# Attention feeding a SwiGLU block: four half steps of the third tile ahead of the first tile's outputs, activations in five half buffers, one v scale behind the weight casts

## The chip, the cores and the metric

One Trainium2 chip, one of its cores. The metric is the device time of one execution of the whole kernel, in microseconds (us). Every program is run several times; a profiled execution is one more run whose instructions were recorded.

## The reference

Two parts follow each other. First, a decaying linear attention over 4 sequences of 768 positions with 8 heads of width 64. It goes block by block; every block of a sequence needs the state that the block before it has left. Second, a gated feed-forward block over the 3072 x 512 result.

```python
for b in range(nb):                                   # blocks of one sequence, in order
    intra = einsum('bhic,bhjc->bhij', qb, kb) * Dmask  # decay lam ** (i - j), causal
    intra = einsum('bhij,bhjd->bhid', intra, vb)
    inter = einsum('bhid,bhde->bhie', qb * lam_pow, kv_state)
    out[:, :, sl] = intra + inter
    kv_state = lam_block * kv_state + einsum('bhsd,bhse->bhde', kb * rev_pow, vb)
x = out.transpose(0, 2, 1, 3).reshape(3072, 512)
g = x @ w_gate                                        # 512 -> 1536
result = (g * sigmoid(g) * (x @ w_val)) @ w_out       # 1536 -> 512
```

Inputs and output are float32; inside, the kernel works in bfloat16 with float32 accumulation.

## The kernel before

**Tiles and groups.** The 3072 rows are six *tiles* of 512 rows. A tile has two *groups* of 256 rows, so there are twelve groups, g0 to g11; group g belongs to tile g // 2. Attention works by group, the feed-forward block by tile.

**What a group needs.** k, q and v are loaded as float32 (`load_group`, on SyncE's queue SP). `cast_scaled` makes bfloat16 of k on ScalarE (L258) and of q, with its decay, on VectorE (L260), and then issues a transposing DMA on SP (L251). `v_scale` writes v with its decay on GpSimd (L238). `upd_mm` (L382) multiplies scaled v with k on TensorE, `upd_copy` copies the result out of PSUM on ScalarE (tile `ups`, L404), and `state` runs a chain of small additions and copies on GpSimd (L421 to L432) that gives the group its incoming states `kvn` and leaves `kvs` for the next block. `scores` (L326, or L352 from group 6 on) and its masks on VectorE (`ssb`) give the causal part. `core_a` (L461) and `core_b` (L474) accumulate the group's result, and `evac` copies it into the tile's input `xt` (L486), two copies, either one each on VectorE and ScalarE (`SPLIT`) or both on ScalarE, as for groups 4 and 5.

**The feed-forward block.** A *step* (t, fc) takes 128 of the 1536 inner columns of tile t: four matmuls by `w_gate` (L514), a Silu on ScalarE (`sil`, L518), four matmuls by `w_val` (L528) and the product on VectorE (`h`, L531). A step can be a half step: group columns 0:2 or 2:4 alone, matmuls of 256 columns in place of 512. Tile 1 runs as half steps throughout (`s1a`, then `s1b`). `ffn_out(t, b)` makes 128 output rows: twelve matmuls of `h` by `w_out` (L547), a copy to `osb` (L549) and a DMA (L550). The very last one is done in two column slices, so that its copies and DMAs overlap. PSUM is eight banks taken in a ring.

**What sets the order.** It is written out by hand. `steps` lists the steps; `at(n, fn, ...)` hangs work behind step n; the loop at the end emits step after step and what hangs on it. Each engine runs its instructions in that order, and waits at the first whose inputs are not ready. DMAs wait on SP's queue in the same way. `ahead(g)` is `upd` (update matmul, copies, state chain) and `scores` of group g; `attend(g)` is `core_a(g)`, then `upd_mm`, `upd_copy` and `scores` of g + 1, then `core_b(g)`, then the state chain of g + 1.

**Around the change.** `w_out` comes as six pieces; `wo_cast` makes bfloat16 of them (L232), five on GpSimd and the last on ScalarE behind step (1, 10) of `s1b`. On GpSimd the scale of v of group 5 stands ahead of the last of its five casts. After the last step of tile 1 come the four outputs of tile 0 with the attention of group 5 between them; then the steps of tile 2, with `ahead(6)` behind step 2, the cast of group 7 behind step 3, its v scale behind step 4, `attend(6)` behind step 6, the cast of group 8 behind step 7, `attend(7)` behind step 10, and the outputs of tile 1 behind steps 0, 3, 7 and 9.

Of the kernel before, what the change touches and what calls it, by code (L numbers as in the profile page):

```python
# [9 lines left out]
BF16 = mybir.dt.bfloat16  # L10
# [9 lines left out]
@with_exitstack  # L20
def kernel(
    ctx: ExitStack,
    tc: tile.TileContext,
    q: bass.AP,
    k: bass.AP,
    v: bass.AP,
    lam: bass.AP,
    moe_w_gate: bass.AP,
    moe_w_val: bass.AP,
    moe_w_out: bass.AP,  # L30
    out: bass.AP,
):
    nc = tc.nc
    with tc.manual_schedule():
        _body(ctx, tc, nc, q, k, v, lam, moe_w_gate, moe_w_val, moe_w_out, out)


def _body(ctx, tc, nc, q, k, v, lam, moe_w_gate, moe_w_val, moe_w_out, out):
    B, H, S, D = q.shape
    HP = H // 2  # L40
    BLK = 128
    NBLK = S // BLK
    DM = H * D
    DFF = moe_w_gate.shape[1]
    MC = DM // 128
    FC = DFF // 128
    NG = NBLK * B // 2
    M = BLK // 2

# [8 lines left out]
    PB = B // 2  # L58
    groups = [(t % PB * 2 + j, t // PB) for t in range(NG // 2) for j in range(2)]

# [6 lines left out]
    vs_pool = ctx.enter_context(tc.tile_pool(name="vs", bufs=4))  # L67
    ssb_pool = ctx.enter_context(tc.tile_pool(name="ssb", bufs=2))
    xt_pool = ctx.enter_context(tc.tile_pool(name="xt", bufs=2))
    h_pool = ctx.enter_context(tc.tile_pool(name="h", bufs=2))  # L70
    sil_pool = ctx.enter_context(tc.tile_pool(name="sil", bufs=3))
    osb_pool = ctx.enter_context(tc.tile_pool(name="osb", bufs=3))
    kv_pool = ctx.enter_context(tc.tile_pool(name="kv", bufs=1))
# [5 lines left out]
    def bank():  # L79
        b = banks[ring[0] % 8]  # L80
        ring[0] += 1
        return b
# [8 lines left out]
    st = {}  # L91
# [54 lines left out]
    for b2 in range(2):  # L146
        ps = slice(b2 * M, b2 * M + M)
# [4 lines left out]
    for b2 in range(2):  # L152
        ps = slice(b2 * M, b2 * M + M)
# [46 lines left out]
    wv_sb = wpool.tile([128, MC, DFF], BF16, name="wv_sb")  # L200
    wo_sb = wpool.tile([128, FC, DM], BF16, name="wo_sb")
    wg_d = moe_w_gate.rearrange("(c p) f -> p c f", p=128)
# [163 lines left out]
    def upd_mm(g, up=None):  # L366
        b, i = groups[g]
        v_s = st[("vs", g)]
        up = up or [bank() for _ in range(2)]
        started = set()  # L370
        for s in range(2):
            for hp in range(HP):
                for r in range(2):
                    if g >= NAT0 and i == NG // B - 1 and 2 * s + r == 3:
                        continue
                    for h2 in range(2):
                        ps = slice(r * M, r * M + M)
                        h = 2 * hp + h2
                        if g >= NAT0 and r:
                            h = H - 1 - h  # L380
                        n = hp + (HP * s if g >= NAT0 else 0)
                        nc.tensor.matmul(up[r][h2 * 64:h2 * 64 + 64, n * D:n * D + D],  # L382
                                         st[("qk", g)][ps, 0, s, h * D:h * D + D],
                                         v_s[ps, 2 * hp + h2, s],
                                         start=(r, h2) not in started, stop=(s == 1 or g >= NAT0),
                                         skip_group_check=True)
                        started.add((r, h2))
        st[("up", g)] = up

    def upd_copy(g, parts=(0, 1)):  # L390
# [10 lines left out]
        for r in range(2):  # L401
            n = HP * D if g < NAT0 or (r == 1 and i == NG // B - 1) else 2 * HP * D
            u = kv_pool.tile([128, 2 * HP * D], FP32, name="ups", tag="ups", bufs=4)
# [6 lines left out]
    def state(g):  # L410
        b, i = groups[g]
        last = i == NG // B - 1
        us = st[("ups", g)]
# [76 lines left out]
    def core_a(g):  # L490
        st[("op", g)] = [bank() for _ in range(2)]
        inter(g, True)
        guard(g)

    def core_b(g, fns=(nc.scalar.copy, nc.scalar.copy)):
        run_later(len(later))
        intra(g, False)
        evac(g, fns)
# [19 lines left out]
        nc.scalar.activation(sil[:, 0:N], gp[:, 0:N], AF.Silu)  # L518

    def ffn_val(t, fc, b0=0, b1=B):  # L520
        if ("h", t) not in st:
            st[("h", t)] = h_pool.tile([128, FC, B, BLK], BF16, name="h", tag="h")
        h_sb, xt, sil = st[("h", t)], st[("xt", t)], st[("sil", t, fc, b0)]
        N = (b1 - b0) * BLK
        fs = slice(fc * 128, fc * 128 + 128)
        vp = bank()
        for mc in range(MC):
            nc.tensor.matmul(vp[:, 0:N], wv_sb[:, mc, fs],  # L528
                             xt[:, b0 // 2:b1 // 2, mc].rearrange("p g b n -> p g (b n)"),
                             start=(mc == 0), stop=(mc == MC - 1))  # L530
        nc.vector.tensor_tensor(out=h_sb[:, fc, b0:b1].rearrange("p b n -> p (b n)"),  # L531
                                in0=sil[:, 0:N], in1=vp[:, 0:N], op=ALU.mult)

    def ffn_fc(t, fc, b0=0, b1=B):
        ffn_gate(t, fc, b0, b1)
        ffn_val(t, fc, b0, b1)

    def ffn_out(t, b, last=False):
        h_sb = st[("h", t)]
        osb = osb_pool.tile([128, DM], FP32, name="osb", tag="osb")  # L540
        row = groups[2 * t + b // 2][0] * S + (groups[2 * t + b // 2][1] * 2 + b % 2) * BLK
        halves = ((0, DM // 2, nc.scalar.copy, nc.scalar), (DM // 2, DM, nc.vector.tensor_copy, nc.sync)) \
            if last else ((0, DM, nc.scalar.copy, nc.scalar),)
        for c0, c1, fn, eng in halves:
            ps = bank()[:, 0:c1 - c0]
            for fc in range(FC):
                nc.tensor.matmul(ps, h_sb[:, fc, b], wo_sb[:, fc, c0:c1],  # L547
                                 start=(fc == 0), stop=(fc == FC - 1))
            fn(out=osb[:, c0:c1], in_=ps)  # L549
            eng.dma_start(out=bass.AP(tensor=out.tensor, offset=out.offset + row * DM + c0,  # L550
                                      ap=[[DM, 128], [1, c1 - c0]]),
                          in_=osb[:, c0:c1])
# [6 lines left out]
    def attend(g):  # L559
        run_later(len(later))  # L560
        core_a(g)
        if g + 1 < NG:
            upd_mm(g + 1)
# [3 lines left out]
        core_b(g)  # L567
        if g + 1 < NG:
            later[:] = late
# [80 lines left out]
    inter(1, False)  # L650
    evac(1, SPLIT)
    ffn_val(0, 0, 0, 2)
    ring[0] = 6
    ffn_gate(0, 1, 0, 2)
    ffn_gate(0, 0, 2, 4)
    w_piece(6, 8)
    w_cast()
    ring[0] = 4
    ffn_val(0, 0, 2, 4)
    ffn_val(0, 1, 0, 2)  # L660
    ring[0] = 2
# [9 lines left out]
    def step(t, fc, b0=0, b1=B):  # L671
        steps.append((t, fc, b0, b1))
        return len(steps) - 1

    def at(n, fn, *a):
        plan.setdefault(n, []).append((fn, a))

    s0 = {fc: step(0, fc) for fc in range(2, FC - 1)}
    s0["11a"], s0["11b"] = step(0, FC - 1, 0, 2), step(0, FC - 1, 2, 4)
    at(s0[2], w_cast)  # L680
# [3 lines left out]
    at(s0[3], swapped_q_table)  # L684
    at(s0[4], w_cast)
    at(s0[4], state, 1)
    at(s0[4], load_group, 2, "v")
    at(s0[5], load_group, 3)
    at(s0[6], w_cast)
    at(s0[7], load_group, 4, "kq")  # L690
# [2 lines left out]
    at(s0[8], pe_transpose, 2, 0)  # L693
    at(s0[8], pe_transpose, 2, 1)
    at(s0[8], w_cast)
    at(s0[8], v_scale, 2, nc.gpsimd)
    at(s0[9], scores, 2)
    at(s0[9], run_later, 4)
    at(s0[10], upd_mm, 2)
# [8 lines left out]
    s1b = [step(1, fc, 2, 4) for fc in range(FC)]  # L708
# [19 lines left out]
    at(s1b[6], run_later, 2)  # L728
    at(s1b[6], wo_cast)
    at(s1b[6], wo_cast)  # L730
    at(s1b[6], v_scale, 5, nc.gpsimd)
    at(s1b[8], wo_cast)
    at(s1b[9], core_a, 4)
    at(s1b[10], core_b, 4)
    at(s1b[10], wo_cast, ACTC)
    at(s1b[11], ffn_out, 0, 0)
    at(s1b[11], ahead, 5)
    at(s1b[11], run_later, 3)
    at(s1b[11], ffn_out, 0, 1)
    at(s1b[11], core_a, 5)  # L740
    at(s1b[11], ffn_out, 0, 2)
    at(s1b[11], core_b, 5)
    at(s1b[11], cast_scaled, 6)
    at(s1b[11], load_group, 7)
    at(s1b[11], v_scale, 6, nc.gpsimd)
    at(s1b[11], ffn_out, 0, 3)

    outs = [(1, b) for b in range(4)]
    for t in range(2, NG // 2):
        sn = [step(t, fc) for fc in range(FC)]  # L750
        if t == 2:
            at(sn[2], ahead, 6)
        for j, g in ((3 if t == 2 else 0, 2 * t + 3), (7 if t == 2 else 6, 2 * t + 4)):
            if g < NG:
                at(sn[j], cast_scaled, g)
                if g + 1 < NG:
                    at(sn[j], load_group, g + 1)
                at(sn[1 + j], v_scale, g, nc.gpsimd)
        if t + 1 < NG // 2:
            at(sn[6 if t == 2 else 4], attend, 2 * t + 2)  # L760
            at(sn[10], attend, 2 * t + 3)
        for n, o in zip((0, 3, 7, 9), outs):
            at(sn[n], ffn_out, *o)
        outs = [(t, b) for b in range(4)]

# [40 lines left out]
```

## Time and profile before

| | us |
|---|---|
| median of 5 runs | 228.33 |
| lowest and highest of them | 227.96 and 229.51 |
| the profiled execution's own time | 228.64 |
| its span, from the first to the last instruction | 226.9 |
| busy in that span: TensorE | 219.3 |
| ScalarE | 107.2 |
| GpSimd | 89.9 |
| VectorE | 89.2 |

A profile line names the engine (PE is TensorE, PEld its weight loads, ACT ScalarE, DVE VectorE, POOL GpSimd, SP SyncE, with a q for the queue that issues DMAs), the source line, and the tiles it writes and reads. A timeline line has the start and the length in us first, then how many instructions it merges (x4), and in brackets the idle time of the engine before it and what ended that. The lengths of matmuls overlap, since they are pipelined: the distance from one start to the next is the better measure. The profiled execution lies 0.31 us above the median, and 1.74 us of its time lie outside the span.

### The profile page before, as it was taken

To read this page: it belongs to the slowest core of one execution; us is meant where nothing else is said; L and a number is where in the kernel's file an instruction comes from. 1 tells how busy PE (TensorE), PEld (TensorE's weight loads), DVE (VectorE), ACT (ScalarE), POOL (GpSimd) and SP (SyncE) were. 2 spreads that over 40 slices of the span, in tenths; PEclk is the share of its full clock that TensorE was granted. 3 is DMA by queue.
4 is the path that set the end of the run, shared out by engine and by line. 5 is a ranking of instruction groups with operands and counts; after the bars stand their busy time and mean duration, and the time that the engine had idled before them with its cause. 6 is when DMAs were issued, how large, how long until landed. Compare 5 with 4: busy or idle time off the path is not lost.

```text
span 226.9 us, 5902 instructions
## 1 busy us (share of the span) xinstructions
PE 219.3 (97%) x2443; PEld 118.4 (52%) x2443; DVE 89.2 (39%) x151; ACT 107.2 (47%) x209; POOL 89.9 (40%) x131
## 2 busy tenths in 40 slices
PE   8889999999998999999999999999999999999994
PEld 3556455878864444454544544544544444444443
DVE  2664357685834214444253262253242123222200
ACT  6868585754662446364454453453533423322221
POOL 6676747642795303977463092192150000000000
PEclk9999999999999999999999999999999999999999
DMA  6999999899997678878988749915101101101122
GB/s 195 344 360 376 367 336 326 218 248 301 342 259 187 190 173 211 192 178 203 216 182 185 187 98 208 223 33 139 49 3 48 46 3 46 46 0 46 49 92 92
DMA packets 88013, 39.70 MB, mean 175 GB/s; under 512 B 57651, under 2 KB 83507, under 8 KB 87987
## 3 DMA queue, kind: packets, MB, share of 16 engines
q1 hardware_dynamic: 83474, 32.64, 54.6%
q10 hardware_dynamic: 4512, 6.69, 8.2%
q8 instruction: 19, 0.31, 0.6%
q14 instruction: 8, 0.06, 0.1%
HBM read 28.31 MB, written 6.29 MB: 152 GB/s over the span
## 4 chain that ended last, share of the span: by engine, by line
PE 82%; DMA 5%; SPq 5%; POOL 5%; issue 1%; ACT 0%; DVE 0%; DVEq 0%; POOLq 0%
PE bank L547 27%; PE bank L514 25%; PE bank L528 24%; SPq L99 4%; DMA woraw<-in_moe_w_out_dram 3%; DMA v<-in_v_dram 2%; POOL wo_sb L232 2%; POOL v_s L238 2%; PE bank L474 2%; PE bank L461 2%; PE bank L382 1%; PE bank L352 1%; SPq L227 1%; POOL kvf L421 1%; PE bank L326 0%
## 5 line engine op out<-in xcount | busy, mean ns | idle before, releaser
L531 DVE TENSOR_TENSOR h<-sil,bank 128x512 bf16<-128x512 bf16 (+1 forms) x87 | 51.4, 595 | 107.5 <-PE bank L528 92.4
L514 PE MATMUL bank<-xt,wg_sb 128*128 128x512 bf16 (+1 forms) x348 | 76.6, 343 | 0.0
L528 PE MATMUL bank<-xt,wv_sb 128*128 128x512 bf16 (+1 forms) x348 | 76.4, 342 | 0.0
L518 ACT ACTIVATE sil<-bank 128x512 bf16<-128x512 f32 (+1 forms) x87 | 45.9, 527 | 44.3 <-PE bank L514 41.3
L547 PE MATMUL bank<-wo_sb,h 128*128 128x512 bf16 (+1 forms) x300 | 65.8, 371 | 0.9 <-POOL wo_sb L232 0.9
L528 PEld LDWEIGHTS <-wv_sb 128*128 128x128 bf16 x348 | 34.0, 98 | 28.3
L547 PEld LDWEIGHTS <-h 128*128 128x128 bf16 x300 | 29.1, 98 | 33.5 <-issue 1.2
L514 PEld LDWEIGHTS <-wg_sb 128*128 128x128 bf16 x348 | 32.4, 98 | 27.2 <-DVE xt L486 0.3
L549 ACT COPY osb<-bank 128x512 f32<-128x512 f32 (+1 forms) x24 | 13.9, 578 | 54.3 <-PE bank L547 52.3
L238 POOL TENSOR_TENSOR v_s<-v,dec 128x1024 bf16<-128x1024 f32 (+1 forms) x14 | 23.3, 1668 | 14.0 <-DMA v<-in_v_dram 11.1
L421 POOL TENSOR_TENSOR kvf<-kvs,ups 128x256 f32<-128x256 f32 x8 | 5.8, 728 | 43.7 <-ACT ups L404 42.4
L333 DVE TENSOR_TENSOR ssb<-bank,causal 128x512 bf16<-128x512 f32 x24 | 15.3, 683 | 4.0 <-PE bank L326 3.8
L486 ACT CAST xt<-bank 128x512 bf16<-128x512 f32 x21 | 12.8, 664 | 2.9 <-PE bank L474 2.5
L421 POOL TENSOR_TENSOR kvf<-kvf,ups 128x256 f32<-128x256 f32 x16 | 12.6, 787 | 0.6
L430 POOL CAST kvn<-kvf 64x256 bf16<-64x256 f32 x24 | 11.6, 482 | 1.5
L404 ACT COPY ups<-bank 128x256 f32<-128x256 f32 (+1 forms) x24 | 9.5, 449 | 2.3 <-PE bank L382 1.4
L258 ACT CAST qk<-kraw 128x1024 bf16<-128x1024 f32 x9 | 9.4, 1040 | 0.6 <-DMA kraw<-in_k_dram 0.6
L260 DVE TENSOR_TENSOR qk<-qraw,qdn 128x1024 bf16<-128x1024 f32 x6 | 7.4, 1236 | 5.6 <-DMA qraw<-in_q_dram 5.6
L357 DVE TENSOR_TENSOR ssb<-bank,causaln 128x512 bf16<-128x512 f32 x12 | 8.2, 687 | 1.2 <-PE bank L352 1.1
L232 POOL CAST wo_sb<-woraw 128x1024 bf16<-128x1024 f32 x5 | 6.0, 1218 | 5.5 <-DMA woraw<-in_moe_w_out_dram 5.5
L221 POOL CAST wv_sb<-wraw 128x1024 bf16<-128x1024 f32 (+1 forms) x6 | 5.8, 971 | 5.0 <-DMA wraw<-in_moe_w_val_dram 4.9
L474 PE MATMUL bank<-ssb,v_s 64*64 64x128 bf16 (+1 forms) x384 | 6.8, 208 | 0.5 <-ACT guard L445 0.5
(63 smaller groups left out, 118.8 us busy)
## 6 DMA issues: line engine op xcount, KB each, us to landing
out_dram<-osb ACTq DMA_DIRECT2D x23, 256.0 KB, 2.0
v<-in_v_dram SPq DMA_DIRECT2D x16, 256.0 KB, 4.6
woraw<-in_moe_w_out_dram SPq DMA_DIRECT2D x6, 512.0 KB, 7.1
kraw<-in_k_dram SPq DMA_DIRECT2D x24, 128.0 KB, 3.4
qraw<-in_q_dram SPq DMA_DIRECT2D x24, 128.0 KB, 3.6
wraw<-in_moe_w_gate_dram SPq DMA_DIRECT2D x5, 512.0 KB, 6.6
wraw<-in_moe_w_val_dram SPq DMA_DIRECT2D x5, 512.0 KB, 6.9
kraw<-in_k_dram SPq DMA_DIRECT2D x4, 512.0 KB, 7.0
```

Source lines behind the costliest of these rows:

```text
L238: eng.tensor_tensor(out=st[("vs", g)][:, h0:h1], in0=st[("v", g)][:, h0:h1].rearrange("p h (s d) -> p h s d", s=2), in1=vfac(g, h0, h1), o ...
L333: nc.vector.tensor_tensor(out=ssb[:, h2, 2 * c:2 * c + 2].rearrange("p a s n -> p a (s n)"), in0=sp[(c, h2)].rearrange("p (a x) -> p a x", ...
L421: nc.gpsimd.tensor_tensor(out=o, in0=f, in1=u, op=ALU.add)
L430: nc.gpsimd.tensor_copy(out=o[64 - h2 * 64:128 - h2 * 64], in_=f[h2 * 64:h2 * 64 + 64])
L474: nc.tensor.matmul(op[r][h2 * 64:h2 * 64 + 64, cols(g, hp, s)], v_s[ps, 2 * hp + h2, s], ssb[ps, h2, hp * 2 + s] if g >= NAT0 else ssb[ps, ...
L486: fns[r](out=xt[:, g % 2, :, r].rearrange("p h (m s) -> p h s m", s=2) if g < NAT0 else xt[:, g % 2, :, :, r * M:r * M + M], in_=op[r].rea ...
L514: nc.tensor.matmul(gp[:, 0:N], wg_sb[:, mc, fs], xt[:, b0 // 2:b1 // 2, mc].rearrange("p g b n -> p g (b n)"), start=(mc == 0), stop=(mc = ...
L518: nc.scalar.activation(sil[:, 0:N], gp[:, 0:N], AF.Silu)
L528: nc.tensor.matmul(vp[:, 0:N], wv_sb[:, mc, fs], xt[:, b0 // 2:b1 // 2, mc].rearrange("p g b n -> p g (b n)"), start=(mc == 0), stop=(mc = ...
L531: nc.vector.tensor_tensor(out=h_sb[:, fc, b0:b1].rearrange("p b n -> p (b n)"), in0=sil[:, 0:N], in1=vp[:, 0:N], op=ALU.mult)
L547: nc.tensor.matmul(ps, h_sb[:, fc, b], wo_sb[:, fc, c0:c1], start=(fc == 0), stop=(fc == FC - 1))
L549: fn(out=osb[:, c0:c1], in_=ps)
```

## The change

- **The activations `h`** are kept in half tiles of six inner blocks each, five buffers of them, instead of two whole tiles.
- **Four half steps of tile 2**, (2, 0) to (2, 3) for group 4's columns 0:2, are emitted right behind the last step of tile 1, and the outputs of tile 0 with the attention of group 5 hang behind the last of them. When tile 2's own steps come, its first four are half steps for columns 2:4.
- **Within tile 2** the work hangs elsewhere: `ahead(6)` behind step 4 (it was 2), the cast of group 7 behind 4 (3), its v scale behind 5 (4), `attend(6)` behind 7 (6), the cast of group 8 behind 8 (7), its v scale behind 9 (8); `attend(7)` stays behind 10; the outputs of tile 1 behind 1, 5, 7 and 9 (0, 3, 7, 9).
- **The v scale of group 5** on GpSimd stands behind the fifth weight cast instead of ahead of it.
- **v of group 2** is loaded and scaled in two halves of four heads.
- **The very last output** is sliced 384 and 128 columns instead of 256 and 256.

```diff
+    FH = FC // 2
-    h_pool = ctx.enter_context(tc.tile_pool(name="h", bufs=2))
+    h_pool = ctx.enter_context(tc.tile_pool(name="h", bufs=5))
...
-        if ("h", t) not in st:
-            st[("h", t)] = h_pool.tile([128, FC, B, BLK], BF16, name="h", tag="h")
+        hn = ("h", t, fc // FH)
+        if hn not in st:
+            st[hn] = h_pool.tile([128, FH, B, BLK], BF16, name="h", tag="h")
...
-        halves = ((0, DM // 2, nc.scalar.copy, nc.scalar), (DM // 2, DM, nc.vector.tensor_copy, nc.sync)) \
+        halves = ((0, DM - 128, nc.scalar.copy, nc.scalar), (DM - 128, DM, nc.vector.tensor_copy, nc.sync)) \
...
-    at(s0[4], load_group, 2, "v")
+    at(s0[4], load_fp32, 2, nc.sync, v, "v", 0, H // 2)
+    at(s0[4], load_fp32, 2, nc.sync, v, "v", H // 2, H)
...
-    at(s0[8], v_scale, 2, nc.gpsimd)
+    at(s0[8], v_scale, 2, nc.gpsimd, 0, H // 2)
+    at(s0[8], v_scale, 2, nc.gpsimd, H // 2, H)
...
-    at(s1b[6], v_scale, 5, nc.gpsimd)
     at(s1b[8], wo_cast)
+    at(s1b[8], v_scale, 5, nc.gpsimd)
     at(s1b[9], core_a, 4)
     at(s1b[10], core_b, 4)
     at(s1b[10], wo_cast, ACTC)
-    at(s1b[11], ffn_out, 0, 0)
-    at(s1b[11], ahead, 5)
...
+    NH = 4
+    s2 = [step(2, fc, 0, 2) for fc in range(NH)][-1]
+    at(s2, ffn_out, 0, 0)
+    at(s2, ahead, 5)
...
-        sn = [step(t, fc) for fc in range(FC)]
+        sn = [step(t, fc, 2 if t == 2 and fc < NH else 0) for fc in range(FC)]
         if t == 2:
-            at(sn[2], ahead, 6)
-        for j, g in ((3 if t == 2 else 0, 2 * t + 3), (7 if t == 2 else 6, 2 * t + 4)):
+            at(sn[4], ahead, 6)
+        for j, g in ((4 if t == 2 else 0, 2 * t + 3), (8 if t == 2 else 6, 2 * t + 4)):
...
-            at(sn[6 if t == 2 else 4], attend, 2 * t + 2)
+            at(sn[7 if t == 2 else 4], attend, 2 * t + 2)
             at(sn[10], attend, 2 * t + 3)
-        for n, o in zip((0, 3, 7, 9), outs):
+        for n, o in zip((1, 5, 7, 9) if t == 2 else (0, 3, 7, 9), outs):
```

More of the change, by code (lines that the diff above doesn't have):

```diff
@@ L520, in ffn_val @@
     def ffn_val(t, fc, b0=0, b1=B):
-        if ("h", t) not in st:
-            st[("h", t)] = h_pool.tile([128, FC, B, BLK], BF16, name="h", tag="h")
-        h_sb, xt, sil = st[("h", t)], st[("xt", t)], st[("sil", t, fc, b0)]
+        hn = ("h", t, fc // FH)
+        if hn not in st:
+            st[hn] = h_pool.tile([128, FH, B, BLK], BF16, name="h", tag="h")
+        h_sb, xt, sil = st[hn], st[("xt", t)], st[("sil", t, fc, b0)]
         N = (b1 - b0) * BLK
@@ L530, in ffn_val @@
                              start=(mc == 0), stop=(mc == MC - 1))
-        nc.vector.tensor_tensor(out=h_sb[:, fc, b0:b1].rearrange("p b n -> p (b n)"),
+        nc.vector.tensor_tensor(out=h_sb[:, fc % FH, b0:b1].rearrange("p b n -> p (b n)"),
                                 in0=sil[:, 0:N], in1=vp[:, 0:N], op=ALU.mult)
@@ L538, in ffn_out @@
     def ffn_out(t, b, last=False):
-        h_sb = st[("h", t)]
         osb = osb_pool.tile([128, DM], FP32, name="osb", tag="osb")
         row = groups[2 * t + b // 2][0] * S + (groups[2 * t + b // 2][1] * 2 + b % 2) * BLK
-        halves = ((0, DM // 2, nc.scalar.copy, nc.scalar), (DM // 2, DM, nc.vector.tensor_copy, nc.sync)) \
+        halves = ((0, DM - 128, nc.scalar.copy, nc.scalar), (DM - 128, DM, nc.vector.tensor_copy, nc.sync)) \
             if last else ((0, DM, nc.scalar.copy, nc.scalar),)
@@ L546, in ffn_out @@
             for fc in range(FC):
-                nc.tensor.matmul(ps, h_sb[:, fc, b], wo_sb[:, fc, c0:c1],
+                nc.tensor.matmul(ps, st[("h", t, fc // FH)][:, fc % FH, b], wo_sb[:, fc, c0:c1],
                                  start=(fc == 0), stop=(fc == FC - 1))
@@ L735, in _body @@
     at(s1b[10], wo_cast, ACTC)
-    at(s1b[11], ffn_out, 0, 0)
-    at(s1b[11], ahead, 5)
[L738 to L746, printed above, removed]
+    NH = 4
+    s2 = [step(2, fc, 0, 2) for fc in range(NH)][-1]
+    at(s2, ffn_out, 0, 0)
+    at(s2, ahead, 5)
+    at(s2, run_later, 3)
+    at(s2, ffn_out, 0, 1)
+    at(s2, core_a, 5)
+    at(s2, ffn_out, 0, 2)
+    at(s2, core_b, 5)
+    at(s2, cast_scaled, 6)
+    at(s2, load_group, 7)
+    at(s2, v_scale, 6, nc.gpsimd)
+    at(s2, ffn_out, 0, 3)
     outs = [(1, b) for b in range(4)]
     for t in range(2, NG // 2):
-        sn = [step(t, fc) for fc in range(FC)]
+        sn = [step(t, fc, 2 if t == 2 and fc < NH else 0) for fc in range(FC)]
         if t == 2:
-            at(sn[2], ahead, 6)
-        for j, g in ((3 if t == 2 else 0, 2 * t + 3), (7 if t == 2 else 6, 2 * t + 4)):
+            at(sn[4], ahead, 6)
+        for j, g in ((4 if t == 2 else 0, 2 * t + 3), (8 if t == 2 else 6, 2 * t + 4)):
             if g < NG:
```

## The prediction

> **What bounds the kernel now.** I read the page first: its busy shares and its chain.
>
> ```profile
> PE 219.3 (97%) x2443; PEld 118.4 (52%) x2443; DVE 89.2 (39%) x151; ACT 107.2 (47%) x209; POOL 89.9 (40%) x131
> PE 82%; DMA 5%; SPq 5%; POOL 5%; issue 1%; ACT 0%; DVE 0%; DVEq 0%; POOLq 0%
> PE bank L547 27%; PE bank L514 25%; PE bank L528 24%; SPq L99 4%; DMA woraw<-in_moe_w_out_dram 3%; DMA v<-in_v_dram 2%; POOL wo_sb L232 2%; POOL v_s L238 2%; PE bank L474 2%; PE bank L461 2%; PE bank L382 1%; PE bank L352 1%; SPq L227 1%; POOL kvf L421 1%; PE bank L326 0%
> ```
>
> TensorE is busy 97% and is 82% of the chain; the rest of the chain is the start and one detour over the cast of `w_out` (`wo_sb`, L232). The granted clock is full in all 40 slices. From 15 us on, start to start, a 512-column matmul takes 216 ns and a 256-column one 109 ns, so only three things can change the time: TensorE's waits, its extra instructions, and the tail. The timeline of TensorE around the detour, then GpSimd and ScalarE there:
>
> ```profile
> 65.21 0.61 PE L514 MATMUL bank<-xt,wg_sb 128*128 128x256 bf16 x4
> 66.09 1.89 PE L547 MATMUL bank<-wo_sb,h 128*128 128x512 bf16 x8
> 68.88 1.02 PE L547 MATMUL bank<-wo_sb,h 128*128 128x512 bf16 x4 [0.90 <-POOL wo_sb L232]
> 63.94 2.03 POOL L232 CAST wo_sb<-woraw 128x1024 bf16<-128x1024 f32 x2
> 65.93 1.92 POOL L238 TENSOR_TENSOR v_s<-v,dec 128x1024 bf16<-128x1024 f32 x1
> 67.79 1.04 POOL L232 CAST wo_sb<-woraw 128x1024 bf16<-128x1024 f32 x1
> 65.34 1.33 ACT L486 CAST xt<-bank 128x512 bf16<-128x512 f32 x2 [0.59 <-PE bank L474]
> ```
>
> The first output's twelve matmuls run from 66.09 to 69.83, 3.74 us; the second's take 2.69 (70.66 to 73.35). So the wait costs **1.05 us**. It is the fifth cast, held back by the v scale of group 5.
>
> The second place is group 7's scaled v, in tile 2:
>
> ```profile
> 87.65 0.45 PE L382 MATMUL bank<-v_s,qk 64*64 64x64 bf16 x32
> 88.86 0.72 POOL L421 TENSOR_TENSOR kvf<-kvs,ups 128x256 f32<-128x256 f32 x1 [9.04 <-ACT ups L404]
> 91.53 1.31 DVE L260 TENSOR_TENSOR qk<-qraw,qdn 128x1024 bf16<-128x1024 f32 x1
> 91.73 1.70 POOL L421 TENSOR_TENSOR kvf<-kvf,ups 128x256 f32<-128x256 f32 x1
> 96.26 1.91 POOL L238 TENSOR_TENSOR v_s<-v,dec 128x1024 bf16<-128x1024 f32 x1
> 98.23 0.46 PE L382 MATMUL bank<-v_s,qk 64*64 64x64 bf16 x32
> 92.99 2.02 SPq L251 DMA_TRANSPOSE qkt<-qk  x1
> ```
>
> The update of group 6 (87.65) releases GpSimd's state chain (88.86), behind which the v scale of group 7 is queued; it ends at 98.17. TensorE's update of group 7 needs it and starts at 98.23. There is no slack: 10.58 us lie between the two updates, and GpSimd needs 10.52 of them. The trace has group 7's transpose landing at 97.89, against its scores at 98.51: 0.6 us of slack.
>
> **The change, part by part.**
>
> *Weight wait, -1.05.* Behind the state chain GpSimd now does three casts, 63.94 + 3 x 1.0 = 66.95, and ScalarE's piece ends at 67.57. The outputs start some 4 us later than before, so nothing of the wait is left. The v scale of group 5 then ends at 68.85; its user, the update of group 5, comes at 73.
>
> *New wait for `xt`, +0.64.* The first half step of tile 2 reads group 4's `xt`. TensorE is free at 66.09; ScalarE makes both copies and ends at 65.34 + 1.33 = 66.67. Group 3's evacuation shows that TensorE goes on 0.06 after the last copy (copies end at 53.24, gate starts at 53.30). So it starts at 66.73. Bounds 0.5 and 0.8. Before, this copy was hidden beside the first output. Queued behind the wait on TensorE is everything else, the outputs too.
>
> *Half steps, +0.09.* Eight half steps are 16 quartets of 256-column matmuls at 0.4375 us, 7.00; the four whole steps that they replace are 8 quartets at 0.864, 6.91. The added Silus and products (0.38 and 0.42 us a half) lie on engines that are busy 47% and 39%: free, as long as they keep to TensorE's 0.875 us per half step, which they do in tile 1.
>
> *Half buffers, 0.* Going round five buffers, tile 2's second half gets tile 0's first, whose outputs are all done before; no writer meets a reader.
>
> *v of group 2 in halves, 0.* SP issues one DMA more, some 0.7 us, in a stretch where the DMA engines are over 90% busy anyway. The v scale ended near 36.6, the update of group 2 started at 36.93: 0.3 us of slack, and half loads let the first half start sooner. Bounds -0.05 and +0.3, taken 0. The later weight loads have over 2 us of slack once the outputs start later.
>
> *Group 7's wait, +1.69.* This decides. Between the updates of groups 6 and 7 stood four steps and one output; now three steps and one output: 10.58 - 1.73 = 8.85 us. GpSimd's ten steps and the v scale are the same and start on the same copy of `ups`, so v is ready 10.52 us after the update of group 6, and TensorE waits 1.67 to 1.7 us there. All that is queued on TensorE waits with it. There is a second floor under it. Group 7's loads are issued behind group 6's transpose, which waits for a k cast behind the evacuation of group 5 on ScalarE; that moves by the net of the work moved ahead: 4 x 0.875 + 0.64 - 1.05 = 3.1 us later. So q of group 7, whose last piece landed at 91.35, lands at 94.5; VectorE's cast ends at 95.8 (92.84 before), and the transpose, 5.05 us from the cast's end, lands at 100.9. By my count TensorE gets to tile 2's own steps at 82.9, to the update of group 6 at 90.8 and would be at the scores of group 7 at 99.9: it would wait 1.0 us even if v were ready. The two overlap, so it is the larger, 1.69; bounds 0.7 (below) and 2.0.
>
> The lower bound comes from the collision in the rows: the addition at 91.73 took 1.70 us against 0.72 for the first, while VectorE's q cast ran. Without that 0.98, v would be ready at 9.54 and the wait 0.7. The Trainium skill, page "SBUF — State Buffer", section "Who interferes with whom", says that a VectorE instruction with two SBUF inputs and a GpSimd one that reads SBUF exclude each other, the one that starts first going through whole. By it the cast, moved 3 us into the chain, would again hold GpSimd up, for at most its own 1.22 us.
>
> By the rows alone I take the collision as staying, since the cast's new time, 94.5 to 95.8, is again inside the chain, which runs from 92.0 to 99.4.
>
> *The same at group 8, +0.5.* Between the updates of groups 7 and 8 there is also one step less, and group 8's loads follow group 7's transpose, 3 us later, on SP. TensorE after its wait is 3.1 later at the update of group 7 and 1.4 later at that of group 8. The v of group 8 is ready at 112.7, its user comes at 113.2: covered. The q cast now waits for the product of step 8 and a mask, and ends at 109.4; transposes land 4.4 to 5.5 us after the cast (groups 8 and 9), so at 113.8 to 114.9, and the scores want it at 113.4. Bounds 0 and 1.2; I take 0.5, near group 8's own transpose. Group 9 has 4 us of slack or more.
>
> *Tail, -0.2.* The rows:
>
> ```profile
> 222.28 0.37 ACT L549 COPY osb<-bank 128x256 f32<-128x256 f32 x1 [0.72 <-PE bank L547]
> 223.64 0.42 DVE L549 COPY osb<-bank 128x256 f32<-128x256 f32 x1 [9.69 <-DMA out_dram<-osb]
> 224.09 0.38 SPq L550 DMA_DIRECT2D out_dram<-osb  x1
> 31.97 0.89 PE bank L289 x16
> ```
>
> TensorE's sum stays: 12 x 162 + 12 x 56 = 2.62 us, as 24 x 109 before (56 from the 128-column transposes at L289, 0.89 / 16; 162 between the sizes). VectorE's copy of half the columns saves 0.13 (0.69 at 512, 0.42 at 256). The last DMA has half the bytes; 256 KB land in 2.0 us and 128 KB in 1.76, so 0.1 less. ScalarE's larger slice is under way 0.5 us earlier and stays hidden. Bounds -0.3 and +0.1.
>
> The Trainium skill speaks against this slice: page "TensorE: Matmul & The Clock Gate", section "Back-to-back issue gap", has about 81 ns per 128-column matmul where weights are loaded for each. By it the last twelve would take 12 x 25 = 0.3 us more, an estimate, and the tail would be +0.1. The rows, 56 ns with weight loads in between, say otherwise.
>
> **Sum.** -1.05 + 0.64 + 0.09 + 1.69 + 0.5 - 0.2 = +1.67 us. Against the profiled execution, 228.64, that is 230.3; against the median, 0.31 lower, **230.0 us**, 0.7% slower. A measurement of this kernel can tell about 0.5%, 1.14 us: below 227.19 counts as faster, above 229.47 as slower.
>
> **The rivals.**
>
> *Forecast (0.60):* both new waits of tile 2 come, 229.5 to 230.9.
>
> *A, not slower (0.15): group 7's wait isn't there.* Place: the update of group 7. It decides if v is ready 8.85 us after the update of group 6 instead of 10.52: GpSimd without the collision (0.98 less), and 0.7 more. Sum without the two waits of tile 2: -1.05 + 0.64 + 0.09 - 0.2 = -0.52, so 227.8; down to 227.1 if the copy of `xt` is hidden as well. For it: spans on GpSimd are rough. Against: the update at 98.23 follows 0.06 behind the scale's end.
>
> *B, half of it (0.17):* the v scale is 1 us early, or the transpose decides, and group 8's wait stays away. -0.52 + 0.7 to 1.6: 228.5 to 229.4, no difference that can be told.
>
> *C, more (0.08):* transposes take 5.5 us and group 8 waits over 1 us, or v of group 8 lands late: 231 to 231.5.
>
> That the change doesn't remove the weight wait I hold for excluded: the casts end 2.7 us before the outputs start.
>
> **How the numbers follow.** The likeliest case gives 230.0. The range 228.3 to 231.0 takes in the forecast and B, and leaves out most of A and C. Slower: the forecast and C, 0.68. Faster: the lower end of A, 0.04. Same: the rest, 0.28.
>
> **What would show it.** Right: no wait on `wo_sb`; the gate of (2, 0) some 0.6 us behind the last step of tile 1, released by ScalarE's `xt`; the update of group 7 right behind the end of its v scale, 10.5 us after the update of group 6, with 1.7 us idle on TensorE before it; a shorter wait at the scores of group 8. Wrong: TensorE without a gap there, or the GpSimd chain from update to scaled v under 9.5 us; then A or B holds. A wait anywhere before 65 us would mean that the halved v load costs something.

## The result, and the profile after

| | before | after |
|---|---|---|
| median, us | 228.62 (79 runs) | 229.57 (44 runs) |
| lowest, us | 227.77 | 229.22 |
| profiled execution, us | 228.64 | 229.36 |
| its span, us | 226.94 | 227.62 |

The ratio of after to before is 1.0045, interval 1.0033 to 1.0058: 1.03 us slower (0.75 to 1.33). The interval leaves out no change, but 0.45% lies just under the 0.5% that the prediction had set as its bound, so by that bound it is "the same", and the likeliest class (slower by more) was missed narrowly. The forecast time, 230.0, lies 0.4 above the median. It was counted from the 228.33 of the first five runs of before; over all 79 before lies at 228.62.

The page of after, busy shares and chain, then its first wait lines (in all, times, longest):

```profile
PE 218.8 (96%) x2475; PEld 120.5 (53%) x2475; DVE 89.6 (39%) x155; ACT 107.7 (47%) x213; POOL 89.9 (39%) x132
PE 79%; POOL 7%; issue 6%; SPq 3%; DMA 2%; ACT 1%; ACTq 0%; DVE 0%; POOLq 0%; DVEq 0%
```

```profile
PE bank L383 <- POOL v_s L239: 1.7, 1, 1.7
...
PE bank L515 <- ACT xt L487: 0.5, 1, 0.5
```

The lines are shifted by one or two against before. GpSimd has 7% of the chain where it had 5%, and the cast of `wo_sb` has left it: `v_s` and `kvf` have grown (3% and 2%, from 2% and 1%), and `kvs` and `kvn` have come. The 6% under "issue" are mostly one piece, GpSimd's idle time ahead of the state chain of group 6 (79.72 to 91.36), in which TensorE was busy. The wait on `wo_sb` is gone from the list; one on `v_s` stands first, and one on `xt` is new. The timeline of TensorE, then GpSimd and ScalarE, around the first outputs:

```profile
65.11 0.60 PE L530 MATMUL bank<-xt,wv_sb 128*128 128x256 bf16 x4
66.16 0.60 PE L515 MATMUL bank<-xt,wg_sb 128*128 128x256 bf16 x4 [0.45 <-ACT xt L487]
69.65 2.75 PE L548 MATMUL bank<-wo_sb,h 128*128 128x512 bf16 x12
72.33 0.45 PE L383 MATMUL bank<-v_s,qk 64*64 64x64 bf16 x32
63.53 3.02 POOL L233 CAST wo_sb<-woraw 128x1024 bf16<-128x1024 f32 x3
66.50 1.92 POOL L239 TENSOR_TENSOR v_s<-v,dec 128x1024 bf16<-128x1024 f32 x1
64.78 1.33 ACT L487 CAST xt<-bank 128x512 bf16<-128x512 f32 x2 [0.58 <-PE bank L475]
```

The three casts end at 66.55, the outputs begin at 69.65, and the first takes 2.68 us to the next instruction. In its place the gate of (2, 0) waits until both copies of `xt` are done (66.11): 1.05 us from the last val quartet to it, where a quartet needs 0.44.

The same for group 7: GpSimd and VectorE, then TensorE.

```profile
91.41 0.73 POOL L422 TENSOR_TENSOR kvf<-kvs,ups 128x256 f32<-128x256 f32 x1 [11.68 <-ACT ups L405]
93.92 1.45 POOL L433 CAST kvn<-kvf 128x256 bf16<-128x256 f32 x1
98.88 1.91 POOL L239 TENSOR_TENSOR v_s<-v,dec 128x1024 bf16<-128x1024 f32 x1
93.88 1.22 DVE L261 TENSOR_TENSOR qk<-qraw,qdn 128x1024 bf16<-128x1024 f32 x1 [2.19 <-DMA qraw<-in_q_dram]
90.19 0.45 PE L383 MATMUL bank<-v_s,qk 64*64 64x64 bf16 x32
97.78 1.03 PE L530 MATMUL bank<-xt,wv_sb 128*128 128x512 bf16 x4
100.84 0.44 PE L383 MATMUL bank<-v_s,qk 64*64 64x64 bf16 x32 [1.65 <-POOL v_s L239]
101.09 0.47 PE L353 MATMUL bank<-qkt 64*64 64x64 bf16 x32
```

TensorE has finished its steps and `core_a` and stands still until the scale of v ends at 100.79. From update to update it is 10.65 us, nearly what it was before (10.58), with one step fewer in between.

Laying the distances between the same instructions of the two executions side by side shows where the time went (us; the distance is from start to start; the third column is the work that the change moved into or out of the stretch, from quartets of 0.4375 and 0.864):

| stretch | before | after | moved work | what is left |
|---|---|---|---|---|
| second half of step (1, 11) to first output | 0.88 | 4.99 | +3.50 | +0.61 |
| first output to update of group 5 | 3.74 | 2.68 | 0 | -1.06 |
| update of group 5 to update of group 6 | 17.82 | 17.86 | +0.05 | -0.01 |
| update of group 6 to update of group 7 | 10.58 | 10.65 | -1.73 | +1.80 |
| update of group 7 to last output | 122.54 | 120.85 | -1.73 | +0.04 |
| last output to end | 6.17 | 5.93 | 0 | -0.24 |
| sum | 161.73 | 162.96 | +0.09 | +1.14 |

The sum is +1.23. The spans differ by only 0.68, because this execution of after reached step (1, 11) 0.55 us earlier. All of that arises in the first 15.2 us, ahead of anything that the change touches, so it belongs to the execution and not to the kernel.

The rows of group 8 in after (VectorE, SyncE's queue, TensorE), then the end of the kernel:

```profile
107.70 1.42 DVE L261 TENSOR_TENSOR qk<-qraw,qdn 128x1024 bf16<-128x1024 f32 x1
109.26 1.64 SPq L252 DMA_TRANSPOSE qkt<-qk  x1
112.63 0.42 PE L383 MATMUL bank<-v_s,qk 64*64 64x64 bf16 x24
113.05 0.45 PE L353 MATMUL bank<-qkt 64*64 64x64 bf16 x32
224.57 0.29 DVE L550 COPY osb<-bank 128x128 f32<-128x128 f32 x1 [9.69 <-DMA out_dram<-osb]
224.89 0.37 SPq L551 DMA_DIRECT2D out_dram<-osb  x1
```

### The profile page after: what moved, and what is told of

Its sections match the earlier page's. It is cut to its first block, busy times and chain, and to the rows that moved or that the text cites. A ratio compares the mean times of both kernels' runs of the same rounds, so it can differ in the third digit from the quotient of the medians.

```text
span 227.6 us, 5984 instructions
## 1 busy us (share of the span) xinstructions
PE 218.8 (96%) x2475; PEld 120.5 (53%) x2475; DVE 89.6 (39%) x155; ACT 107.7 (47%) x213; POOL 89.9 (39%) x132
## 4 chain that ended last, share of the span: by engine, by line
PE 79%; POOL 7%; issue 6%; SPq 3%; DMA 2%; ACT 1%; ACTq 0%; DVE 0%; POOLq 0%; DVEq 0%
PE bank L515 26%; PE bank L530 25%; PE bank L548 22%; POOL v_s L239 3%; SPq L100 2%; DMA v<-in_v_dram 2%; PE bank L475 2%; POOL kvf L422 2%; PE bank L462 2%; PE bank L383 1%; POOL kvs L425 1%; POOL kvn L433 1%; PE bank L327 1%; PE bank L353 1%; POOL kvn L431 1%
## 5 line engine op out<-in xcount | busy, mean ns | idle before, releaser
L548 PE MATMUL bank<-wo_sb,h 128*128 128x512 bf16 (+2 forms) x300 | 65.7, 371 | 0.0
L530 PEld LDWEIGHTS <-wv_sb 128*128 128x128 bf16 x364 | 35.4, 98 | 26.9 <-POOL wv_sb L222 0.3
L515 PEld LDWEIGHTS <-wg_sb 128*128 128x128 bf16 x364 | 34.0, 98 | 26.7 <-issue 0.6
L548 PEld LDWEIGHTS <-h 128*128 128x128 bf16 x300 | 28.6, 98 | 32.5
L422 POOL TENSOR_TENSOR kvf<-kvf,ups 128x256 f32<-128x256 f32 x16 | 11.6, 725 | 0.6
L233 POOL CAST wo_sb<-woraw 128x1024 bf16<-128x1024 f32 x5 | 5.1, 1044 | 6.6 <-DMA woraw<-in_moe_w_out_dram 6.6
```

The costliest lines, as they stand in the source:

```text
L422: nc.gpsimd.tensor_tensor(out=o, in0=f, in1=u, op=ALU.add)
L515: nc.tensor.matmul(gp[:, 0:N], wg_sb[:, mc, fs], xt[:, b0 // 2:b1 // 2, mc].rearrange("p g b n -> p g (b n)"), start=(mc == 0), stop=(mc = ...
L530: nc.tensor.matmul(vp[:, 0:N], wv_sb[:, mc, fs], xt[:, b0 // 2:b1 // 2, mc].rearrange("p g b n -> p g (b n)"), start=(mc == 0), stop=(mc = ...
L548: nc.tensor.matmul(ps, st[("h", t, fc // FH)][:, fc % FH, b], wo_sb[:, fc, c0:c1], start=(fc == 0), stop=(fc == FC - 1))
```

## The experiments

The names of the kernels: *before* and *after* are those above; every experiment is one of the two with the edit shown.

**The v scale of group 5 alone (before, one line moved).**

```diff
-    at(s1b[6], v_scale, 5, nc.gpsimd)
     at(s1b[8], wo_cast)
+    at(s1b[8], v_scale, 5, nc.gpsimd)
```

> The kernel before, with one part of the change alone: the v scale of group 5 stands behind the fifth weight cast on GpSimd. My theory: the weight wait (1.05 us) was only this order, so it goes without any half step. The fifth cast ends at 66.95 instead of 68.83, while the first output reaches it at 66.09 + 8 x 0.216 = 67.8; the v scale ends at 68.85, and the update of group 5 wants it at 68.8, so at most 0.1 us comes back. Time -1.0 us against the kernel before, ratio 0.9956. Rival, that the half steps are what hides the wait: the ScalarE piece or the loads hold the output up as before, ratio 0.999 to 1.0.

Measured: 228.01 us, ratio 0.9979 (0.9953 to 1.0005). TensorE's timeline and SyncE's queue:

```profile
66.42 2.54 PE L547 MATMUL bank<-wo_sb,h 128*128 128x512 bf16 x11
69.40 0.45 PE L382 MATMUL bank<-v_s,qk 64*64 64x64 bf16 x32 [0.44 <-POOL v_s L238]
70.76 0.64 PE L326 MATMUL bank<-qkt 64*64 64x128 bf16 x32 [0.92 <-DMA qkt<-qk]
58.87 8.23 SPq L251 DMA_TRANSPOSE qkt<-qk  x1
```

The weight wait is gone with this one line. In the profiled execution two waits have taken part of its place: the update of group 5 for the moved v scale (0.44), and its scores for the transpose (0.92), which landed at 70.72. The theory had at most 0.1 us coming back; the ratio came out at 0.9979 instead of 0.9956, which the interval still holds. This execution (229.38 us) also lies 1.37 us above the kernel's median, so its waits need not be the usual ones. In before neither made TensorE wait: the v scale ended at 67.85 and the transpose landed at 68.46, ahead of the update at 69.83. The row of that transpose on SyncE lasts 6.16 us in before and 4.77 to 8.23 over all kernels here. Kernels that are the same up to the last output differ in it too: 6.16 in before against 7.82 with the tail alone, 8.23 here against 4.77 in the best of the parts. So its landing varies by execution.

**The other way round: after, with the v scale of group 5 back ahead of the fifth cast.**

```diff
+    at(s1b[6], v_scale, 5, nc.gpsimd)
     at(s1b[8], wo_cast)
-    at(s1b[8], v_scale, 5, nc.gpsimd)
```

> The changed kernel with the v scale of group 5 back ahead of the fifth weight cast, as before. Theory: the four half steps alone hide the cast: they move the outputs from 66.1 to about 70.7 us, and the fifth cast would end near 68.9. No wait on wo_sb, the update of group 5 not held up, and a time within 0.1 us of the changed kernel, 0.45% above the kernel before (ratio 1.0045). Rival: the weight wait comes back in part: a wait on wo_sb of 0.3 us or more, ratio 1.006 or more.

Measured: 229.42 us, 0.15 below after's median; ratio 1.0018 (0.9991 to 1.0046), which just holds the 1.0045 of after, but no change as well. The time alone settles little; the trace does. The fifth cast now ends at 68.09:

```profile
67.05 1.04 POOL L233 CAST wo_sb<-woraw 128x1024 bf16<-128x1024 f32 x1
69.94 2.75 PE L548 MATMUL bank<-wo_sb,h 128*128 128x512 bf16 x12
```

That is still 1.85 us ahead of the outputs. So each of the two parts removes the weight wait by itself: beside the half steps the new place of the v scale brings nothing, and without them it is enough.

**v of group 7 scaled on VectorE (after).**

```diff
-                at(sn[1 + j], v_scale, g, nc.gpsimd)
+                at(sn[1 + j], v_scale, g, nc.vector if g == 7 else nc.gpsimd)
```

> The changed kernel, with the v scale of group 7 on VectorE instead of GpSimd, so that it does not stand behind the state chain of group 6. My theory has two floors under the update and scores of group 7: the v scale (ready 10.6 us after the update of group 6) and the transpose, which landed at 100.4. With the first gone TensorE waits at the scores instead of the update, for 1.0 to 1.2 us instead of 1.8: 0.6 to 0.8 us less than the changed kernel, ratio to the kernel before about 1.0015. Rival, the v scale alone was late: 1.8 us less, ratio 0.9965. Rival, the half steps and moved positions cost by themselves: ratio unchanged, 1.0045.

**The loads of group 7 ahead of group 6's transpose (after).**

```diff
-    at(s2, cast_scaled, 6)
     at(s2, load_group, 7)
+    at(s2, cast_scaled, 6)
```

> The changed kernel, with the loads of group 7 issued on SP ahead of the transpose of group 6 instead of behind it; nothing else moves. My theory: the loads and with them the q cast and the transpose of group 7 come 2 to 4 us earlier, but the v scale still stands behind the state chain, 10.6 us after the update of group 6, so TensorE waits as long as before at the update of group 7 (1.7 to 1.9 us): ratio to the kernel before unchanged, 1.0045 (1.0035 to 1.005). Rival, the loads of group 7 were the cause: the wait goes, 1.8 us less, ratio 0.9965.

**Both of them.**

> The changed kernel with both: the v scale of group 7 on VectorE, and the loads of group 7 ahead of the transpose of group 6. My theory of two floors, of which the later one counts: each alone leaves the other (0.9 us were left at the scores with the v scale moved), both together take the whole wait of 1.8 us away. Update of group 7 some 8.85 us after that of group 6, ratio to the kernel before 0.997. Rival, a third floor (the state copies, or VectorE, which now has a scale and a cast in a row): 0.5 us or more of idle stays, ratio above 0.999.

Measured:

| | median | ratio (interval) | update 6 to update 7 | idle at update of g7 | idle at scores of g7 |
|---|---|---|---|---|---|
| after | 229.57 | 1.0045 (1.0033, 1.0058) | 10.65 | 1.83 | 0 |
| v on VectorE | 228.66 | 1.0013 (0.9982, 1.0044) | 8.81 | 0 | 0.90 |
| loads first | 229.59 | 1.0050 (1.0032, 1.0069) | 10.48 | 1.66 | 0 |
| both | 228.22 | 0.9995 (0.9976, 1.0014) | 8.81 | 0 | 0 |

Here idle is the distance to the next instruction beyond what the same group takes undisturbed. The timeline of TensorE with v on VectorE, then with both:

```profile
99.39 0.49 PE L383 MATMUL bank<-v_s,qk 64*64 64x64 bf16 x32
100.56 0.45 PE L353 MATMUL bank<-qkt 64*64 64x64 bf16 x32 [0.68 <-DMA qkt<-qk]
```

```profile
99.31 0.49 PE L383 MATMUL bank<-v_s,qk 64*64 64x64 bf16 x32
99.62 0.56 PE L353 MATMUL bank<-qkt 64*64 64x64 bf16 x32
```

With the loads first, TensorE, GpSimd and VectorE:

```profile
101.08 0.45 PE L383 MATMUL bank<-v_s,qk 64*64 64x64 bf16 x32 [1.49 <-POOL v_s L239]
92.60 1.73 POOL L431 CAST kvn<-kvf 64x256 bf16<-64x256 f32 x2
92.02 1.60 DVE L261 TENSOR_TENSOR qk<-qraw,qdn 128x1024 bf16<-128x1024 f32 x1
```

These four kernels settle group 7. There are two floors, one above the other. Taking the lower one away (loads first) moves nothing: the transpose then landed at 97.43 and TensorE still waits 1.66 us for v. Taking the upper one away gives 0.91 us by the medians and lets the lower one show, 0.90 us. Only with both gone is the whole wait gone. The kernels with one edit came out near the ratios expected of them (1.0015 and 1.0045). The kernel with both did so in the trace, with no idle and 8.81 us, but not by its ratio: 0.9995 against 0.997, which the interval leaves out. The medians give 1.35 us for both edits, less than the 1.83 idle in the trace. The profiled execution with both (227.90) was the fastest of its twelve, 0.32 below their median; what the others lose was not shown. (The medians were taken on several chips, on which before lay between 228.44 and 228.88.)

**Group 4's evacuation on both engines (after).**

```diff
-    at(s1b[10], core_b, 4)
+    at(s1b[10], core_b, 4, SPLIT)
```

> The changed kernel, with the two copies of group 4 into xt made one each by VectorE and ScalarE. My theory: both are done 0.75 us after the last attention matmul instead of 1.35, so the gate of step (2, 0) follows the last step of tile 1 with under 0.1 us of idle instead of 0.61, and the whole is 0.55 us shorter than the changed kernel: ratio to the kernel before about 1.002. Rival, the wait only moves on, to the casts of the weights or to group 7: ratio 1.0035 to 1.0045.

Measured: 228.93 us, ratio 1.0002 (0.9983 to 1.0020), 0.64 below after. TensorE:

```profile
65.06 0.61 PE L515 MATMUL bank<-xt,wg_sb 128*128 128x256 bf16 x4
66.00 0.61 PE L515 MATMUL bank<-xt,wg_sb 128*128 128x256 bf16 x4
```

There is no bracket on the second line: from last step to first output it is 4.45 us instead of 4.99, and all distances behind that stay. The wait on `xt` was worth nearly its full length, 0.54 of the 0.61 us in the traces.

**All three mends at once (after).**

> The changed kernel with the v scale of group 7 on VectorE, the loads of group 7 ahead of the transpose of group 6, and group 4's two copies into xt one each by VectorE and ScalarE. My theory: all three new waits go, 0.55 + 1.8 + 0.1 us, so 2.4 us less than the changed kernel: about 227.1, ratio to the kernel before 0.994 to 0.995. Rival: the gains overlap, because what starts earlier waits for loads or transposes that do not, ratio 0.997 or more.

Measured: 228.52 us, ratio 0.9977 (0.9953 to 1.0001): the theory's 0.994 to 0.995 is out, its rival holds. TensorE:

```profile
89.94 0.44 PE L383 MATMUL bank<-v_s,qk 64*64 64x64 bf16 x32
91.33 0.45 PE L353 MATMUL bank<-qkt 64*64 64x64 bf16 x32 [0.95 <-DMA qkt<-qk]
```

The waits on `xt` and at group 7 are gone, but the scores of group 6 now wait for their own group's transpose, which stands behind the loads of group 7 on SyncE. TensorE comes to the update of group 6 at 89.94, 0.56 us earlier than in the kernel with both edits, where nothing waited; and the issue row of the transpose ended at 87.99, against 86.15 there. The kernel with the loads first alone, in which TensorE is not earlier, has 87.98, so the later issue does not need the split; why the kernel with both edits has less stays open, with one profile of each. With the loads behind the transpose, in after, that row ends at 85.21.

**v of group 7 on VectorE and the split evacuation, loads as in the change (after).**

> The changed kernel with the v scale of group 7 on VectorE and the evacuation of group 4 shared by ScalarE and VectorE; the order of the loads as in the change. Theory: the two earlier gains, 0.91 us and 0.64 us by medians (0.82 and 0.54 in the traces), add, since nothing else is moved on the queue: 228.0 to 228.2 us, ratio 0.9975 to 0.9985. The scores of group 7 still wait 0.9 us for their transpose. Rival: an earlier start of tile 2 only lengthens a wait on a transpose further on: the wait at the scores of group 7 grows to 1.3 us or a new one appears, and the ratio stays at 1.000 or above.

Measured: 228.04 us, the median that the theory had; the ratio, 0.9966 (0.9932 to 1.0000), is a little lower than its 0.9975 to 0.9985, which the interval holds. The two gains add once nothing is moved on the queue. TensorE at group 7:

```profile
98.89 0.49 PE L383 MATMUL bank<-v_s,qk 64*64 64x64 bf16 x32
99.97 0.45 PE L353 MATMUL bank<-qkt 64*64 64x64 bf16 x32 [0.60 <-DMA qkt<-qk]
```

**The tail alone (before).**

```diff
-        halves = ((0, DM // 2, nc.scalar.copy, nc.scalar), (DM // 2, DM, nc.vector.tensor_copy, nc.sync)) \
+        halves = ((0, DM - 128, nc.scalar.copy, nc.scalar), (DM - 128, DM, nc.vector.tensor_copy, nc.sync)) \
```

> The kernel before, with the last output in slices of 384 and 128 columns alone. My theory from the rows: VectorE's copy takes 0.29 instead of 0.42 us and the last DMA has half the bytes, 0.2 to 0.25 us shorter from the last output's start to the end, ratio 0.999. Rival: the twelve 128-column matmuls at about 70 to 80 ns instead of 56 eat it up, ratio 1.0 to 1.0005.

Measured: 228.29 us, ratio 0.9994 (0.9965 to 1.0023), inconclusive by the times. In the trace the stretch from the last output's start to the end is 5.95 us against 6.17 in before, 0.22 less, as the theory had it.

**v of group 2 in halves alone (before).**

```diff
-    at(s0[4], load_group, 2, "v")
+    at(s0[4], load_fp32, 2, nc.sync, v, "v", 0, H // 2)
+    at(s0[4], load_fp32, 2, nc.sync, v, "v", H // 2, H)
...
-    at(s0[8], v_scale, 2, nc.gpsimd)
+    at(s0[8], v_scale, 2, nc.gpsimd, 0, H // 2)
+    at(s0[8], v_scale, 2, nc.gpsimd, H // 2, H)
```

> The kernel before with v of group 2 loaded and scaled in two halves, and nothing else. Theory: nothing, ratio 1.000 within 0.002, no new wait of TensorE before 65 us. Rival: the additional DMA issue on SyncE delays the loads behind it, so that TensorE waits up to 0.3 us longer for group 2 or later weights: ratio 1.0013 and a line of such a wait in the trace.

Measured: 228.18 us, ratio 0.9984 (0.9957 to 1.0010): no cost. It shows something else, in the weight wait. TensorE in this kernel, then GpSimd, then the same two rows with the tail alone:

```profile
69.68 1.02 PE L547 MATMUL bank<-wo_sb,h 128*128 128x512 bf16 x4 [1.58 <-POOL wo_sb L232]
60.77 1.04 POOL L232 CAST wo_sb<-woraw 128x1024 bf16<-128x1024 f32 x1 [0.21 <-DMA woraw<-in_moe_w_out_dram]
69.30 1.02 PE L547 MATMUL bank<-wo_sb,h 128*128 128x512 bf16 x4 [1.30 <-POOL wo_sb L232]
60.41 1.04 POOL L232 CAST wo_sb<-woraw 128x1024 bf16<-128x1024 f32 x1 [0.21 <-DMA woraw<-in_moe_w_out_dram]
```

The wait is 1.58 us here, 1.30 in the kernel with the tail alone, 0.90 in before. It follows the landing of a weight piece: that cast starts at 60.77, 60.41 and 59.96. Before and the kernel with the tail alone are the same up to the last output, so the 0.40 between these two is the execution's. Here the extra DMA could have a part in it; but of the 1.01 us by which the first piece of `w_out` is issued later than in before (52.67 against 51.66), 0.64 is there already at the load of k of group 2 (21.54 against 20.90), ahead of the edit.

**The best of the parts (before, with the v scale of group 5 behind the casts and the tail's slices).**

> The kernel before with two parts of the change alone, the v scale of group 5 behind the fifth weight cast and the last output in slices of 384 and 128 columns. My theory: the weight wait (1.05) goes, up to 0.4 comes back at the update of group 5 and a wait for the transpose of group 5 (landed 68.5 in the kernel before, 70.7 in the run with the v scale alone) of 0 to 1 us comes at its scores, and the tail saves 0.2: 0.2 to 0.9 us less, ratio 0.996 to 0.999. Rival: without half steps in front the transpose always decides and nothing is won but the tail, ratio 0.999.

Measured: 227.52 us (227.12 to 229.00), ratio 0.9964 (0.9943 to 0.9986), faster than both kernels, against before by less than 0.5%. TensorE around the first outputs:

```profile
66.46 2.54 PE L547 MATMUL bank<-wo_sb,h 128*128 128x512 bf16 x11
68.93 0.45 PE L382 MATMUL bank<-v_s,qk 64*64 64x64 bf16 x32
69.20 0.62 PE L326 MATMUL bank<-qkt 64*64 64x128 bf16 x32
```

No wait is left there; the transpose landed at 68.01 in this execution.

## Why the prediction was right or wrong, point by point

- **Weight wait, -1.05: right** in its size for the profiled execution (-1.06) and in its cause. That nothing is left behind it held too. The text gave both parts of the change a share in this; the runs show that either is enough.
- **The wait for `xt`, +0.64: right**, 0.61, released by ScalarE's copies as named. The split evacuation took 0.54 of it away.
- **Half steps, +0.09: right**, as far as it was measured. The +0.09 in the table is the forecast's own arithmetic; the rows agree with it where no wait lies between. The first four half steps take 3.49 us (66.16 to 69.65) for 3.50, and the stretch from group 5 to group 6 grew by 0.04 for 0.05.
- **Half buffers, 0: right**, as far as the table tells: no stretch has more than 0.04 us left that the waits and the tail do not take up.
- **v of group 2, 0: right**, within what can be told: alone it has a ratio of 0.9957 to 1.0010.
- **Group 7's wait, +1.69: right**, 1.80 in the table, and with both floors as given: v first (it was ready 10.60 us after the update of group 6; 10.52 was forecast), the transpose under it at 0.90 (1.0 forecast, landing 100.9; it landed at 100.44).
- **The collision stays: right.** The cast of `kvn` at 93.92 takes 1.45 us where the same instruction of an earlier group took 0.40 at 61.36, beside VectorE's q cast at 93.88. That is 1.05 more, under the q cast's own 1.22. This agrees with the bound that the prediction worked out from the rule in the Trainium skill, page "SBUF — State Buffer", section "Who interferes with whom". In the kernel with the loads first the cast comes at 92.02 and hits another instruction pair (1.73 against 0.85). So rival A, which needs the chain free of it, had no ground.
- **Group 8, +0.5: wrong**, and the term that was mis-sized. From the update of group 7 to the last output only +0.04 is left beyond the moved step. The q cast ended at 109.12, near the 109.4 forecast, but the transpose landed 3.88 us behind it, at 113.00, and the scores began at 113.05, 0.42 behind their update, so some 0.15 us of wait is all that came. The forecast took 4.4 to 5.5 us from the transposes of groups 8 and 9 in before as the bounds; both were too long. Why the same transpose of group 8 landed 0.5 us sooner after its cast than in before was not shown.
- **Tail, -0.2: right**, -0.24. The last twelve matmuls of 128 columns take 0.83 us from the first start to the last end; with 0.22 for a single one that is 0.61 / 11 = 56 ns from start to start. The Trainium skill, page "TensorE: Matmul & The Clock Gate", section "Back-to-back issue gap", has about 81 ns for these; they do not hold here.
- **The sum, +1.67**, was 0.44 above the trace's +1.23, and group 8's term is about all of that.
- **From the trace to the median** the forecast simply took off 0.31 us. By the ratio after is 1.03 us slower (the medians themselves differ by 0.95, the lowest times by 1.45), and the stretches of the two traces sum to 1.23. The interval of the ratio, 0.75 to 1.33 us, holds the 1.23, so it is not shown that this step failed. There is a reason why it could: one profile had been read as if the wait that it shows were a fixed size. The runs show the weight wait at 0.90, 1.30 and 1.58 us, depending on when a weight piece lands, and group 5's transposes landing from 68.01 to 70.72. The half steps put 3.5 us of work between these landings and their users, so after is free of both. That fits the narrower spread of after (median 0.35 above its lowest, against 0.85 for before), and would make the gain at this place larger in a typical run than in the profiled one. That it accounts for the 0.2 us was not shown: before was profiled only once.

So the outcome lies where the forecast case and rival B meet: of the two waits in tile 2 that the forecast case needs, group 7's came in full, and group 8's stayed away as in B. That the absolute time, 229.57, still falls into the forecast case's 229.5 to 230.9 is luck: counted from the 228.33 that the prediction had for before, 1.03 us more would be 229.36, in the range of B.

## What to carry to other kernels

Work moved ahead to cover a wait is taken from somewhere, and there it was cover too: look at what runs between the same two points after the move, and whether an engine's serial chain is as long as that stretch already. Where two resources are late at the same place, price both floors; mending the lower one alone moves nothing, and mending the upper one pays only down to the lower. When a wait hangs on a DMA, take its size from several executions, and try the smallest part of a change by itself: here one moved line removed the wait that the half steps were paying for.

## What the runs showed of the hardware

- The issue row of one and the same transposing DMA on SyncE, group 5's, lasted between 4.77 and 8.23 us in the thirteen kernels, which all issue it at 58.2 to 59.6 us, 0.5 to 4.0 us behind the issue of the last piece of `w_out`; that of group 7, at 95.26 in after, lasted 1.65. What makes the difference was not tested.
- Wherever the q cast of group 7 ran inside GpSimd's chain, the GpSimd instructions beside it took longer by less than the cast's own length: 0.98 us in before, 1.05 in after, 0.88 with the loads first. The cast itself took 1.31, 1.22 and 1.60 us there.
